# Decode step with attention and a gated MLP, forward and backward, on one core: K windows in slots of their own, transposed copies on ScalarE, larger and nested fill packets

## The chip, the cores and the metric

The kernel runs on one core of a Trainium2 chip. The time is the device time of one execution in microseconds. Before the change the median of three runs is 777.7 us (776.77 to 778.44). One more execution was profiled: it took 777.6 us, and the span of its instructions is 775.8 us.

## What is computed

One token passes through a pre-norm block, and the program returns the output and the gradients of all eight inputs.

```
h  = x + attention(layernorm(x), k_cache, v_cache) @ wo     # 16 heads, 8 KV heads, Dh 256
h2 = h + (layernorm(h) @ w_gate * layernorm(h) @ w_up) @ w_down
attention reads only the last W = 4096 of Sk = 32768 cache rows
outputs: h2, dx, dK, dV (1 x 8 x 32768 x 256 each, bf16), dwq, dwo, dw_gate, dw_up, dw_down
```

dK and dV (out_2 and out_3) are 134 MB each. Only the last 4096 rows of each of the 8 groups hold anything but zero; the other 28,672 rows of each group, 14.7 MB, are zeros, and the program has to write them. In all it moves 330 MB, and 281 MB of that are writes.

## The kernel before, in words

**The zero fills.** Everything the zeros need is a few SBUF partitions that hold zeros. `fill` (L87) writes a flat stretch of DRAM from 16 partitions (32, 36, ... 92) that are read over and over, in packets of `f` elements. All fills of whole regions are issued on SyncE, one after another, by `zero_rows_and_fills` (L108): first a piece from the zeroed tile `odd` in 8 KB packets, then the rest of out_2's first region, then 14 regions. Regions number 6 to 10 (`LONG`, L106) go in packets of `NW` = 14,336 elements, 28 KB; the others in packets of `ZW` = 8192 elements, 16 KB. The very last region (out_3, group 7) is dealt out in portions of its own. `deal(eng, e0, k, n, f)` (L97) has `k` partitions write `n` packets of `f` elements each, and `deal_all` has all 16 do so. SyncE deals three portions: 3 partitions with 14 packets of 16 KB, 16 partitions with 24 packets of 16 KB, and 16 partitions with 8 packets of 1224 elements (2448 bytes). The rest is dealt on GpSimd's queue by `deal_rest`: lap 0 once the output h2 is stored, lap 1 at the very end.

**DMA queues.** SyncE and ScalarE issue hardware-generated DMAs; SyncE's go to the queue that the profile calls q1. All loads of K, V and weights and all stores of results are issued by GpSimd, in the order written, on the software queue q0. Both queues feed the same 16 DMA engines. The framework gives hardware DMAs eight completion semaphores in turn: a DMA issued by SyncE waits until the DMA eight places before it has landed on all the engines it uses.

**Attention forward (L346 to L427).** `BIG` is one large SBUF tile cut into slots of 16 KB per partition. The V windows of groups 0 to 6 have slots 0 to 6; K windows alternate between slots 7 and 8 (`K_SLOT`, L40), and V of group 7 takes the slot of K of group 6. K of groups 0 and 1 and V of groups 0 to 2 are loaded at the start; later K windows are loaded in two halves as the slot comes free (L462). `products` (L346) transposes a window on TensorE, 8 blocks at a time, copies them from PSUM with `evac` and multiplies them by the query; `evac` (L296) alternates between ScalarE and VectorE. `moments(g)` weighs K on VectorE, multiplies on TensorE, and in between runs `scores(g+1)` and `softmax(g+1)`.

**MLP, forward and backward (L429 to L628).** The weights are loaded into slots 7 and 8; w_down comes in four pieces through a buffer of four rows. The loop at L567 turns the gradients of gate and up into rows (`to_rows`), broadcasts them (`evac`) and multiplies them with the weights on VectorE. L620 does the same for dq, with one PSUM buffer.

**dK and dV (L691 to L789).** For each group TensorE makes outer products (L764), `evac` copies them to one of the slot pairs named by `PAIR`, and GpSimd stores the pair. Stores of the weight gradients are made on the side (`during`). After the last pair GpSimd issues `deal_rest(1)`.

Of the kernel before, what the change touches and what calls it, by code (L numbers as in the profile page):

```python
# [8 lines left out]
f32 = mybir.dt.float32  # L9
# [5 lines left out]
D = 448  # L15
NI = 7
# [20 lines left out]
TAIL = 9 * SLOT  # L37
RING = TAIL + 6016
SIZE = RING
K_SLOT = [KS + g % 2 for g in range(G)]  # L40


@with_exitstack
def kernel(
# [10 lines left out]

    oT_f = const.tile([128, 32], f32)
    BIG = const.tile([128, SIZE], bf16)
    x_bf = BIG[0:1, 6 * SLOT:6 * SLOT + D]
    S_.dma_start(out=x_bf, in_=A_x.rearrange("a b d -> (a b) d"))
    go_bf = BIG[0:1, 6 * SLOT + 512:6 * SLOT + 512 + D]  # L60
    S_.dma_start(out=go_bf, in_=grad_out.rearrange("a b d -> (a b) d"))

    def flat_rows(w):
# [39 lines left out]
        fill(FILL, last[used[0]:used[0] + 16 * n * f], ALL, n, f)  # L103
        used[0] += 16 * n * f

    LONG = range(6, 11)  # L106

    def zero_rows_and_fills():  # L108
        f = NW // 4
        S_.dma_start(out=zeros[ALL, :].rearrange("p (n f) -> p n f", f=f), in_=odd[ALL, 0:f].unsqueeze(1).to_broadcast([16, 4, f]))  # L110
        fill(FILL, first[16 * NH * FH:], ALL, (FL - NH * FH) // ZW, ZW)
        for g in range(G):
            for k, o in enumerate((out_2, out_3)):
                if (g, k) not in ((0, 0), (G - 1, 1)):
                    f = NW if 2 * g + k in LONG else ZW
                    fill(FILL, region(o, g), ALL, FL // f, f)
        deal(FILL, 0, 3, 14)
        deal_all(24, ZW)
        deal_all(8, 1224)

    def deal_rest(lap):
        if lap == 0:
            deal(IO, 0, 4, 16, ZL)
            deal(IO, 4, 3, 4, ZL)
            deal(IO, 7, 2, 25, ZL)
            deal(IO, 9, 7, 10, ZL)
        else:
            deal(IO, 0, 5, 2, 512)
            deal(IO, 5, 2, 25)
            deal(IO, 7, 2, 2, 2560)  # L130
            deal(IO, 9, 7, 15)
            assert used[0] == 896 * ZW

    def slot(k):
# [35 lines left out]
    def load_V(g):  # L170
        load_window(Vw[g], A_v_cache, g)

    def load_V_half(g, h):
        t = slice(h * T // 2, (h + 1) * T // 2)
        io_load(Vw[g][:, t, :], A_v_cache[0, g, Sk - W:, :].rearrange("(p t) d -> p t d", t=T)[:, t, :])

    load_K(0)
    load_V(0)
    load_K(1)
    load_V(1)  # L180
    wd_rows = B_w_down.rearrange("(s j m) n -> j s (m n)", s=2, j=128)
    load_V(2)


    ident_bf = const.tile([128, 128], bf16)
# [110 lines left out]
    def evac(out, in_):  # L296
# [3 lines left out]
            V_.tensor_copy(out=out, in_=in_)  # L300
        evac_ctr[0] += 1

    xX = const.tile([128, NI], f32)
    V_.tensor_copy(out=xX[:], in_=rows_to_half(x_bf)[:])
    rstd1, xh1, xf1, xx1 = layernorm(xX[:], "ln1")
# [37 lines left out]
        pk_ctr[0] += 1  # L343
        return ring(k).rearrange("p (i h d) -> p i h d", i=2, h=2)

    def products(pool, x_at, vecT, g, out_ps, q):  # L346
        tr = pool.tile([128, 4, 2, 128], bf16, tag="tr", bufs=2, name="tr")
        for i in range(4):
            for dh in range(2):
                P_.transpose(tr[:, i, dh, :], x_at(g, 4 * q + i)[:, dh * 128:(dh + 1) * 128], ident_bf[:])  # L350
        xt = kt_buf()
        evac(xt, tr[:])
        for i in range(4):
            for dh in range(2):
                P_.matmul(out_ps[:, 4 * q + i, :], lhsT=xt[:, i, dh, :], rhs=vecT[:, 4 * g + dh:4 * g + dh + 3:2],  # L355
                          start=(dh == 0), stop=(dh == 1))
# [6 lines left out]
    def scores(g, q):  # L363
        if q == 0:
            sT[g] = fps.tile([128, T, 2], f32, tag="sT", bufs=2, name="sT")
        products(fps, k_at, qT, g, sT[g], q)

    def softmax(g):
        s = sT[g]
        pmax = small.tile([128, 2], f32, tag="pmax")  # L370
        V_.reduce_max(out=pmax[:], in_=s[:].rearrange("p t h -> p h t"), axis=AX)
        mt = ps.tile([2, 128], f32, tag="tmp", bufs=1)
        P_.transpose(mt[:], pmax[:], ident_f[:])
        gmax = small.tile([2, 1], f32, tag="gmax")
        V_.reduce_max(out=gmax[:], in_=mt[:], axis=AX)
        gd = small.tile([2, 2], f32, tag="gd")
        V_.tensor_scalar(out=gd[:], in0=ident_f[0:2, 0:2], scalar1=gmax[:, 0:1], scalar2=-SCALE, op0=ALU.mult, op1=ALU.mult)
        nb = ps.tile([128, 2], f32, tag="tmp", bufs=1)
        P_.matmul(nb[:], lhsT=one[0:2, 0:1].to_broadcast([2, 128]), rhs=gd[:], start=True, stop=True)
        nbias = small.tile([128, 2], f32, tag="nbias")  # L380
        V_.tensor_copy(out=nbias[:], in_=nb[:])
        e = small.tile([128, T, 2], f32, tag="ef")
        sums = small.tile([128, 2], f32, tag="psums")
        for h in range(2):
            S_.activation(out=e[:, :, h], in_=s[:, :, h], func=ACT.Exp, bias=nbias[:, h:h + 1], scale=SCALE, accum_out=sums[:, h:h + 1])
        rs = small.tile([128, 2], f32, tag="rsum")
        V_.reciprocal(out=rs[:], in_=total(sums[:], 2)[:])
        pf = small.tile([128, T, 2], f32, tag="pp", bufs=2)
        V_.tensor_tensor(out=pf[:], in0=e[:], in1=rs[:].unsqueeze(1).to_broadcast([128, T, 2]), op=ALU.mult)
        V_.tensor_copy(out=pT_all[:, g], in_=pf[:])  # L390
        p_f[g] = pf

    def moments(g):

# [3 lines left out]
        for c in range(T // 2):  # L398
# [16 lines left out]
            if g + 1 < G and 4 <= c < 12:  # L415
                with tc.issue_after(mm.ins):
                    scores(g + 1, c - 4)
                if c == 11:
                    softmax(g + 1)
            if c == 8 and g == G - 2:  # L420
                load_V_half(G - 1, 0)
            if c == 8 and g == G - 1:
                load_wo(0, 9)
        S_.copy(out=Mt[:, g, 0, :], in_=MT[0][:])
# [29 lines left out]

    bc2 = [BIG[:, o:o + F].rearrange("p (i c) -> p i c", i=2) for o in (WD0, WD0 - F)]

    for q in range(8):
        scores(0, q)
    softmax(0)
    for g in range(G):  # L460
        moments(g)
        if g + 2 < G:  # L462
            load_K(g + 2, 2)
        if g + 3 < G - 1:
            load_V(g + 3)
        if g == G - 2:
            load_V_half(G - 1, 1)
        if g == 0:

            go_f = BIG[0:1, 6 * SLOT + 1024:6 * SLOT + 1024 + 2 * D].bitcast(f32)  # L470
            V_.tensor_copy(out=go_f, in_=go_bf)
            t = ps.tile([128, D], f32, tag="tmp", bufs=1)
            P_.matmul(t[:], lhsT=one[0:1, 0:1].to_broadcast([1, 128]), rhs=go_f, start=True, stop=True)
            S_.copy(out=dh2_bc[:], in_=t[:])
    load_wo(9, 32)
    io_load(wg_sb, flat_rows(B_w_gate))

# [80 lines left out]
    for w in range(2):  # L558
        V_.tensor_tensor(out=dgu[:, w, 0:FC], in0=d_hh[:], in1=gu[:, 1 - w, :], op=ALU.mult)

    def to_rows(dst, t, cols, j0):
        for j, c in enumerate(cols):
            P_.matmul(t[:, j, :], lhsT=c, rhs=ident_bf[:, j0:j0 + t.shape[-1]], start=True, stop=True)
        evac(dst, t)

    P2 = const.tile([128, 2, NI], f32)
    for w, w_sb in ((0, wg_sb), (1, wu_sb)):  # L567
        for h in range(4):
            r = small.tile([2, HF // 4], bf16, tag="R", name="r")
            t = ps.tile([2, NI, 32], f32, tag="tmp", bufs=1, name="t")  # L570
            to_rows(r[:].rearrange("s (j m) -> s m j", m=NI), t[:], [dgu[:, w, m::NI] for m in range(NI)], 32 * h)
            for i2 in range(2):
                bc = ps.tile([128, HF // 4], f32, tag="tmp", bufs=1, name="bc")
                P_.matmul(bc[:], lhsT=Par[:, i2:i2 + 128], rhs=r[:], start=True, stop=True)
                evac(bc2[w][:, i2, h * HF // 4:(h + 1) * HF // 4], bc[:])
        wv = w_sb.rearrange("p (i c) -> p i c", i=NI)
        for i in range(NI):
            V_.tensor_tensor_reduce(out=wv[:, i, :], in0=wv[:, i, :], in1=bc2[w][:, i % 2, :], scale=1.0, scalar=0.0,
                                    op0=ALU.mult, op1=ALU.add, accum_out=P2[:, w, i:i + 1])
    dhn = const.tile([128, NI], f32)  # L580
# [7 lines left out]
    for b in range(32):  # L588
        V_.tensor_tensor_reduce(out=wg_sb[:, 0:D], in0=parked.get(b, wo_b(b)), in1=dh_bc[:], scale=1.0, scalar=0.0,  # L589
                                op0=ALU.mult, op1=ALU.add, accum_out=doW[:, b:b + 1])  # L590
    doT_f = small.tile([128, 32], f32, tag="pp", bufs=2, name="doT_f")
    V_.tensor_copy(out=doT_f[:], in_=regroup(doW[:], 1)[:])
    doT = const.tile([128, 32], bf16)
# [25 lines left out]
    rows16(doT, do_rows, 1.0)  # L619
    for b1 in range(0, 16, 4):  # L620
        r = wg_sb[0:2, b1 * 128:b1 * 128 + 512]
        t = ps.tile([2, 4, 128], f32, tag="tmp", bufs=1, name="t")
        to_rows(r.rearrange("s (b c) -> s b c", c=128), t[:], [dq[:, b:b + 17:16] for b in range(b1, b1 + 4)], 0)
        for i2 in range(2):
            bc = ps.tile([128, 512], f32, tag="tmp", bufs=1, name="bc")
            P_.matmul(bc[:], lhsT=Par[:, i2:i2 + 128], rhs=r, start=True, stop=True)
            evac(dq_bc[:, i2, b1 * 128:b1 * 128 + 512], bc[:])
    load_odd(IO)  # L628
# [92 lines left out]
    def dP(s, q):  # L721
        g = SEQ[s]
        if q == 0:
            dps[s] = bps.tile([128, T, 2], f32, tag="dp", name="dp")
        products(bps, v_at, doT, g, dps[s], q)

    def factors(s):
        R_ps = ps.tile([128, 2 * Dh], f32, tag="tmp", bufs=1)
# [94 lines left out]
```

## Time and profile before

| What | Value |
|---|---|
| Profiled execution | 777.6 us, span 775.8 us |
| Median of 3 runs | 777.7 us |
| TensorE busy | 60% of the span |
| VectorE busy | 51% |
| ScalarE busy | 20% |
| Moved by DMA | 330.09 MB, mean 425 GB/s |
| 8 KB packets on q0 (K and V halves) | 1792, median 309 ns |
| 16 KB packets on q1 | 9194, median 611 ns |
| 28 KB packets on q1 | 2688, median 1062 ns |
| Last packet of q0 ends | 769.0 us |
| Last packet of q1 ends | 774.5 us |

Times within the execution are counted from the start of the span. The packet rows come from the trace's records of single DMA packets, the others from the page. "DMA share" in a window is the mean busy share of the 16 DMA engines; it can come out at 1.01, since neighbouring packets of one engine overlap by 3 to 4 ns.

### The profile page before, as it was taken

To read this page: it belongs to the slowest core of one execution; us is meant where nothing else is said; L and a number is where in the kernel's file an instruction comes from. 1 tells how busy PE (TensorE), PEld (TensorE's weight loads), DVE (VectorE), ACT (ScalarE), POOL (GpSimd) and SP (SyncE) were. 2 spreads that over 40 slices of the span, in tenths; PEclk is the share of its full clock that TensorE was granted. 3 is DMA by queue.
4 is the path that set the end of the run, shared out by engine and by line. 5 is a ranking of instruction groups with operands and counts; after the bars stand their busy time and mean duration, and the time that the engine had idled before them with its cause. 6 is when DMAs were issued, how large, how long until landed. Compare 5 with 4: busy or idle time off the path is not lost. (4 is left out here: it accounts for less than half of the span.)

```text
span 775.8 us, 10948 instructions
## 1 busy us (share of the span) xinstructions
PE 468.8 (60%) x4427; PEld 259.6 (33%) x4472; DVE 394.3 (51%) x1179; ACT 155.5 (20%) x268; POOL 42.2 (5%) x86
## 2 busy tenths in 40 slices
PE   3899998998996423041326839686958977360000
PEld 2755565555553121020323414232313333030000
DVE  5277766766774121146683526464646756980000
ACT  0211222122110000021003414243423433130000
POOL 2000000000000000010001000000000100001000
PEclk9999999999999755555555555555555555555555
DMA  9999999999999999999999999999999999999998
GB/s 362 429 426 429 425 427 429 427 425 427 428 424 429 433 428 430 436 437 430 427 432 428 431 428 433 428 429 424 432 430 429 431 428 429 429 430 432 431 429 349
DMA packets 22803, 330.09 MB, mean 425 GB/s; under 512 B 2717, under 2 KB 2719, under 8 KB 3992
## 3 DMA queue, kind: packets, MB, share of 16 engines
q1 hardware_dynamic: 12701, 231.17, 69.6%
q0 software_dynamic: 9968, 97.77, 29.9%
q8 instruction: 35, 0.57, 0.3%
q10 hardware_dynamic: 84, 0.46, 0.1%
q14 instruction: 15, 0.12, 0.0%
HBM read 48.33 MB, written 280.59 MB: 424 GB/s over the span
## 5 line engine op out<-in xcount | busy, mean ns | idle before, releaser
L764 PE MATMUL d_ps<-BIG 32*128 32x512 bf16 x256 | 121.4, 598 | 60.2 <-ACT BIG L298 42.8
L407 PE MATMUL MT<-BIG 128*128 128x512 bf16 x467 | 134.5, 394 | 3.8 <-DMA BIG<-in_A_v_cache_dram 1.9
L403 DVE TENSOR_SCALAR BIG<-BIG,pf 128x256 bf16<-128x256 bf16 x512 | 112.6, 280 | 29.9 <-PE MT L407 25.2
L350 PE MATMUL tr<-ident_bf,BIG 128*128 128x128 bf16 x1024 | 113.5, 269 | 20.1 <-DVE doW L589 12.6
L298 ACT CAST BIG<-d_ps 128x512 bf16<-128x512 f32 x156 | 88.4, 588 | 176.8 <-PE d_ps L764 128.3
L350 PEld LDWEIGHTS <-BIG 128*128 128x128 bf16 x1024 | 81.1, 120 | 51.9 <-issue 44.1
L300 DVE COPY BIG<-tr 128x1024 bf16<-128x1024 bf16 x92 | 63.3, 688 | 50.7 <-PE tr L350 50.6
L300 DVE CAST BIG<-d_ps 128x512 bf16<-128x512 f32 x100 | 67.9, 683 | 34.8 <-DMA out_dram<-BIG 28.1
L298 ACT COPY BIG<-tr 128x1024 bf16<-128x1024 bf16 x36 | 36.4, 1012 | 131.6 <-PE tr L350 116.3
L355 PEld LDWEIGHTS <-BIG 128*128 128x128 bf16 x1024 | 36.7, 102 | 70.7 <-DVE BIG L300 44.2
L410 PEld LDWEIGHTS <-BIG 128*128 128x128 bf16 x512 | 42.1, 98 | 44.2 <-issue 8.3
L410 PE MATMUL acc<-pT_all,BIG 128*128 128x2 bf16 x512 | 44.9, 164 | 7.9 <-DVE kbar L427 6.2
L764 PEld LDWEIGHTS <-BIG 32*128 32x128 bf16 x256 | 20.7, 111 | 78.4 <-issue 59.2
L407 PEld LDWEIGHTS <-BIG 128*128 128x128 bf16 x512 | 39.0, 100 | 21.0 <-issue 8.6
L413 PE MATMUL acc<-pT_all,BIG 128*128 128x2 bf16 x512 | 44.2, 164 | 0.0
L413 PEld LDWEIGHTS <-BIG 128*128 128x128 bf16 x512 | 29.9, 96 | 0.9
L528 DVE CUSTOM_DVE_ANT_0 dh_bc<-BIG,dh_bc 128x448 bf16<-128x448 bf16 x14 | 8.7, 624 | 40.5 <-DMA BIG<-in_B_w_down_dram 40.2
L355 PE MATMUL dp<-doT,BIG 128*128 128x2 bf16 x512 | 24.2, 168 | 4.3 <-DVE BIG L300 3.4
L549 PE MATMUL y<-BIG,hh_bf 128*1 128x448 bf16 x14 | 5.9, 564 | 31.5 <-DMA BIG<-in_B_w_down_dram 30.8
L355 PE MATMUL sT<-qT,BIG 128*128 128x2 bf16 x512 | 22.1, 164 | 0.8 <-ACT BIG L298 0.6
L745 DVE TENSOR_TENSOR BIG<-r_ps,mrow 96x1024 bf16<-96x1024 bf16 (+2 forms) x15 | 18.3, 1221 | 1.0 <-PE r_ps L750 0.8
L237 PE MATMUL t<-one,xe 1*128 1x1 f32 x42 | 11.2, 333 | 12.6 <-DVE xe L236 12.6
(190 smaller groups left out, 357.4 us busy)
## 6 DMA issues: line engine op xcount, KB each, us to landing
out_dram<-zeros SPq DMA_DIRECT2D x14, 14336.0 KB, 160.5
out_dram<-BIG POOLq DMA_DIRECT2D x17, 2048.0 KB, 32.4
BIG<-in_A_v_cache_dram POOLq DMA_DIRECT2D x8, 2048.0 KB, 25.2
BIG<-in_A_k_cache_dram POOLq DMA_DIRECT2D x12, 1024.0 KB, 15.0
out_dram<-zeros SPq DMA_DIRECT2D x1, 11264.0 KB, 45.3
out_dram<-zeros SPq DMA_DIRECT2D x1, 6144.0 KB, 81.3
BIG<-in_A_k_cache_dram POOLq DMA_DIRECT2D x2, 2048.0 KB, 24.9
zeros<-in_A_wq_dram SPq DMA_DIRECT2D x1, 3584.0 KB, 15.3
```

The costliest lines, as they stand in the source:

```text
L237: P_.matmul(t[:, i:i + 1], lhsT=c, rhs=one[0:1, 0:1], start=True, stop=True)
L298: S_.copy(out=out, in_=in_)
L300: V_.tensor_copy(out=out, in_=in_)
L350: P_.transpose(tr[:, i, dh, :], x_at(g, 4 * q + i)[:, dh * 128:(dh + 1) * 128], ident_bf[:])
L355: P_.matmul(out_ps[:, 4 * q + i, :], lhsT=xt[:, i, dh, :], rhs=vecT[:, 4 * g + dh:4 * g + dh + 3:2], start=(dh == 0), stop=(dh == 1))
L403: V_.tensor_scalar(out=pk[:, i, h, :], in0=K[:, t, :], scalar1=pf[:, t, h:h + 1], scalar2=None, op0=ALU.mult)
L407: P_.matmul(MT[hf][:], lhsT=v_at(g, t)[:, hf * 128:(hf + 1) * 128], rhs=pk[:, i, :, :].rearrange("p h d -> p (h d)"), start=(t == 0), stop ...
L410: P_.matmul(acc[:, 2 * hf:2 * hf + 2], lhsT=v_at(g, t)[:, hf * 128:(hf + 1) * 128], rhs=pT_all[:, g, t, :], start=(t == 0 and hf == 0), st ...
L413: mm = P_.matmul(acc[:, 4 + dk:7 + dk:2], lhsT=K[:, t, dk * 128:(dk + 1) * 128], rhs=pT_all[:, g, t, :], start=False, stop=(t == T - 1), s ...
L528: V_.tensor_tensor_reduce(out=dh_bc[:], in0=wd_sb[:, m - m0, :], in1=dh2_bc[:], scale=1.0, scalar=0.0, op0=ALU.mult, op1=ALU.add, accum_ou ...
L745: V_.tensor_tensor(out=rows[p0:p1], in0=r_ps[p0:p1, :].unsqueeze(1).to_broadcast([p1 - p0, 8, 128]), in1=mrow[p0:p1, :].unsqueeze(2).to_br ...
L764: mm = P_.matmul(d_ps[:].rearrange("p w d -> p (w d)"), lhsT=rows[32 * k:32 * k + 32, a, :], rhs=R[32 * k:32 * k + 32, :], start=True, sto ...
```

## The change

K of groups 0 to 5 gets slots 3 to 8, one each, and is loaded whole; K of groups 6 and 7 and V of group 7 come in halves, issued in the middle of the moments of group 4, 5 and 6 and after it. x and grad_out, which share a slot at the start, move from slot 6 to slot 8. The copies of K's transposes are all made by ScalarE, as are the copies of the broadcasts of up's gradient; the multiplications there run in reverse order. The dq broadcasts get PSUM buffers of their own (two and four). Region number 5 goes in 28 KB packets. SyncE's last portion, 16 partitions with 8 packets, becomes 16 partitions with 4 packets of 1658 elements, and then 15 DMAs with 15, 14, ... 1 partitions, each with one packet of 256 + 16k elements. Lap 1 of GpSimd's portions carries the same bytes in packets of 25.6 KB and 24 KB. The numbers of elements are the same in all.

```diff
-K_SLOT = [KS + g % 2 for g in range(G)]
+K_SLOT = [3, 4, 5, 6, 7, 8, 7, 8]
...
-    LONG = range(6, 11)
+    LONG = range(5, 11)
...
         deal_all(24, ZW)
-        deal_all(8, 1224)
+        deal_all(4, 1658)
+        for k in range(15, 0, -1):
+            deal(FILL, 0, k, 1, 256 + 16 * k)
...
             deal(IO, 0, 5, 2, 512)
-            deal(IO, 5, 2, 25)
+            deal(IO, 5, 2, 16, 12800)
             deal(IO, 7, 2, 2, 2560)
-            deal(IO, 9, 7, 15)
+            deal(IO, 9, 7, 10, ZL)
...
-    load_V(2)
+    load_K(2)
...
+    def on_act(out, in_):
+        S_.copy(out=out, in_=in_)
...
-        products(fps, k_at, qT, g, sT[g], q)
+        products(fps, k_at, qT, g, sT[g], q, on_act)
...
+    LATE = {4: (Kw[6], A_k_cache, 6), 5: (Kw[7], A_k_cache, 7), 6: (Vw[7], A_v_cache, 7)}
...
+    load_V(2)
+    load_K(3)
+    load_K(4)
     for q in range(8):
         scores(0, q)
...
-        if g + 2 < G:
-            load_K(g + 2, 2)
-        if g + 3 < G - 1:
+        if g < 4:
             load_V(g + 3)
-        if g == G - 2:
-            load_V_half(G - 1, 1)
+        if g in LATE:
+            load_half(*LATE[g], 1)
...
-    for w, w_sb in ((0, wg_sb), (1, wu_sb)):
+    for w, w_sb, ev in ((0, wg_sb, evac), (1, wu_sb, on_act)):
...
-        t = ps.tile([2, 4, 128], f32, tag="tmp", bufs=1, name="t")
+        t = tps.tile([2, 4, 128], f32, tag="qt", bufs=2, name="t")
...
-            bc = ps.tile([128, 512], f32, tag="tmp", bufs=1, name="bc")
+            bc = tps.tile([128, 512], f32, tag="qb", bufs=4, name="bc")
```

More of the change, by code (lines that the diff above doesn't have):

```diff
@@ L57 @@
     BIG = const.tile([128, SIZE], bf16)
-    x_bf = BIG[0:1, 6 * SLOT:6 * SLOT + D]
+    x_bf = BIG[0:1, 8 * SLOT:8 * SLOT + D]
     S_.dma_start(out=x_bf, in_=A_x.rearrange("a b d -> (a b) d"))
-    go_bf = BIG[0:1, 6 * SLOT + 512:6 * SLOT + 512 + D]
+    go_bf = BIG[0:1, 8 * SLOT + 512:8 * SLOT + 512 + D]
     S_.dma_start(out=go_bf, in_=grad_out.rearrange("a b d -> (a b) d"))
@@ L171, in load_V, with load_half @@
         load_window(Vw[g], A_v_cache, g)
-    def load_V_half(g, h):
+    def load_half(dst, cache, g, h):
         t = slice(h * T // 2, (h + 1) * T // 2)
-        io_load(Vw[g][:, t, :], A_v_cache[0, g, Sk - W:, :].rearrange("(p t) d -> p t d", t=T)[:, t, :])
+        io_load(dst[:, t, :], cache[0, g, Sk - W:, :].rearrange("(p t) d -> p t d", t=T)[:, t, :])
     load_K(0)
@@ L344, in pk_buf, with products @@
         return ring(k).rearrange("p (i h d) -> p i h d", i=2, h=2)
-    def products(pool, x_at, vecT, g, out_ps, q):
+    def products(pool, x_at, vecT, g, out_ps, q, ev):
         tr = pool.tile([128, 4, 2, 128], bf16, tag="tr", bufs=2, name="tr")
@@ L351, in products @@
         xt = kt_buf()
-        evac(xt, tr[:])
+        ev(xt, tr[:])
         for i in range(4):
@@ L419, in moments @@
                     softmax(g + 1)
-            if c == 8 and g == G - 2:
-                load_V_half(G - 1, 0)
+            if c == 8 and g in LATE:
+                load_half(*LATE[g], 0)
             if c == 8 and g == G - 1:
@@ L461 @@
         moments(g)
-        if g + 2 < G:
-            load_K(g + 2, 2)
-        if g + 3 < G - 1:
+        if g < 4:
             load_V(g + 3)
-        if g == G - 2:
-            load_V_half(G - 1, 1)
+        if g in LATE:
+            load_half(*LATE[g], 1)
         if g == 0:
-            go_f = BIG[0:1, 6 * SLOT + 1024:6 * SLOT + 1024 + 2 * D].bitcast(f32)
+            go_f = BIG[0:1, 8 * SLOT + 1024:8 * SLOT + 1024 + 2 * D].bitcast(f32)
             V_.tensor_copy(out=go_f, in_=go_bf)
@@ L474 @@
             S_.copy(out=dh2_bc[:], in_=t[:])
+            load_K(5)
     load_wo(9, 32)
@@ L559, with to_rows @@
         V_.tensor_tensor(out=dgu[:, w, 0:FC], in0=d_hh[:], in1=gu[:, 1 - w, :], op=ALU.mult)
-    def to_rows(dst, t, cols, j0):
+    def to_rows(dst, t, cols, j0, ev=evac):
         for j, c in enumerate(cols):
             P_.matmul(t[:, j, :], lhsT=c, rhs=ident_bf[:, j0:j0 + t.shape[-1]], start=True, stop=True)
-        evac(dst, t)
+        ev(dst, t)
     P2 = const.tile([128, 2, NI], f32)
-    for w, w_sb in ((0, wg_sb), (1, wu_sb)):
+    for w, w_sb, ev in ((0, wg_sb, evac), (1, wu_sb, on_act)):
         for h in range(4):
@@ L570 @@
             t = ps.tile([2, NI, 32], f32, tag="tmp", bufs=1, name="t")
-            to_rows(r[:].rearrange("s (j m) -> s m j", m=NI), t[:], [dgu[:, w, m::NI] for m in range(NI)], 32 * h)
+            to_rows(r[:].rearrange("s (j m) -> s m j", m=NI), t[:], [dgu[:, w, m::NI] for m in range(NI)], 32 * h, ev)
             for i2 in range(2):
@@ L574 @@
                 P_.matmul(bc[:], lhsT=Par[:, i2:i2 + 128], rhs=r[:], start=True, stop=True)
-                evac(bc2[w][:, i2, h * HF // 4:(h + 1) * HF // 4], bc[:])
+                ev(bc2[w][:, i2, h * HF // 4:(h + 1) * HF // 4], bc[:])
         wv = w_sb.rearrange("p (i c) -> p i c", i=NI)
-        for i in range(NI):
+        for i in reversed(range(NI)):
             V_.tensor_tensor_reduce(out=wv[:, i, :], in0=wv[:, i, :], in1=bc2[w][:, i % 2, :], scale=1.0, scalar=0.0,
@@ L590 @@
                                 op0=ALU.mult, op1=ALU.add, accum_out=doW[:, b:b + 1])
+    tps_cm.__exit__(None, None, None)
+    tps_cm = tc.tile_pool(name="qps", bufs=1, space=bass.MemoryType.PSUM)
+    tps = tps_cm.__enter__()
     doT_f = small.tile([128, 32], f32, tag="pp", bufs=2, name="doT_f")
@@ L724, in dP @@
             dps[s] = bps.tile([128, T, 2], f32, tag="dp", name="dp")
-        products(bps, v_at, doT, g, dps[s], q)
+        products(bps, v_at, doT, g, dps[s], q, evac)
     def factors(s):
```

## The prediction

> **What bounds the kernel now.** I read the slices of the page first, then the DMA queues, then windows of the last 15 us, then what SyncE waits for. The slices:
>
> ```profile
> DMA  9999999999999999999999999999999999999998
> GB/s 362 429 426 429 425 427 429 427 425 427 428 424 429 433 428 430 436 437 430 427 432 428 431 428 433 428 429 424 432 430 429 431 428 429 429 430 432 431 429 349
> ...
> q1 hardware_dynamic: 12701, 231.17, 69.6%
> q0 software_dynamic: 9968, 97.77, 29.9%
> ```
>
> The 16 DMA engines are busy from end to end, at 424 to 437 GB/s in every slice but the first and the last. TensorE (60%) and VectorE (51%) are not the bound: whenever compute leaves the software queue (q0) empty, the zero fills on q1 take the engines. The time is therefore the packets' sum on each engine, plus some 2 us before the first packet (1.8 us by the packet records), plus what the end adds. The windows show the end (us, TensorE, its weight loads, VectorE, ScalarE, GpSimd, clock, then DMA share and GB/s):
>
> ```profile
> 765.00:767.00 2.00, 0.00 (x0) 0.00 (x0) 0.00 (x0) 0.00 (x0) 0.00 (x0) 0.50 0.98 419
> 767.00:770.00 3.00, 0.00 (x0) 0.00 (x0) 0.00 (x0) 0.00 (x0) 0.00 (x0) 0.50 0.96 410
> 770.00:771.00 1.00, 0.00 (x0) 0.00 (x0) 0.00 (x0) 0.00 (x0) 0.00 (x0) 0.50 0.89 382
> 771.00:772.00 1.00, 0.00 (x0) 0.00 (x0) 0.00 (x0) 0.00 (x0) 0.00 (x0) 0.50 0.82 342
> 772.00:773.00 1.00, 0.00 (x0) 0.00 (x0) 0.00 (x0) 0.00 (x0) 0.00 (x0) 0.50 0.45 182
> 773.00:774.00 1.00, 0.00 (x0) 0.00 (x0) 0.00 (x0) 0.00 (x0) 0.00 (x0) 0.50 0.21 83
> 774.00:775.00 1.00, 0.00 (x0) 0.00 (x0) 0.00 (x0) 0.00 (x0) 0.00 (x0) 0.50 0.03 10
> ```
>
> The share falls in steps: the engines finish one by one. Chaining the packet records engine by engine gives first end 767.1, mean 772.5, last 774.5 us; so perfect balance could save 1.9 us at most. The last three include the engines that carry SyncE's extra 3 x 14 packets. The chain of waits ends at 702.13 us with GpSimd issuing the last fills: compute is over 72 us before the end.
>
> **Packets: minus 0.4 us.** The packet records price a packet by size: 309 ns for 8 KB, 611 for 16, 912 for 24, 1062 for 28. K whole: 1792 packets of 8 KB become 768, so 512 pairs turn into 512 of 16 KB; (2 x 309 - 611) = 7 ns x 512 / 16 engines = 0.22 us. Sixth long region: 896 x 611 - 512 x 1062 = 3.7 us / 16 = 0.23. Lap 1: 25 x 611 - 16 x 950 (between the 24 and 28 KB rows) = 0.08 us on two engines, 15 x 611 - 10 x 912 = 0.05 on seven: 0.03 on average. Four loads fewer save 64 completion packets of 9 ns: 0.04. Sum 0.5; the overlap of 3 to 4 ns per packet takes a quarter back: 0.4 us.
>
> **Compute edits: nothing.** Copies of K's transposes move 32 x 688 ns from VectorE to ScalarE at 1012 ns (the rows of L300 and L298); ScalarE is at 20%. On TensorE, whose waits in the moments stage (40 to 252 us) come to 17 us, K loads account for 4.7 and V for 1.9, so earlier loads gain 7 us of compute at most. In the MLP the last copies of up's gradient no longer queue behind VectorE's products (some 8 us off the compute), and the dq buffers save some 3. Against it, the sixth long region lies beside the w_down pieces: it is next in line after the fill that landed by 289 us, and its own 16 KB packets landed by 326; VectorE waited 40.2 us for these pieces (L528). Where queues alternate, each of a piece's 8 packets per engine would wait 1062 instead of 611 ns, 3.6 us a piece, 7 to 11 in all. Compute thus moves by -18 to +11 us. Its cover is the fills: they keep the engines full either way. After the last issue the software queue still needs about 35 packets of 16 KB per engine, 21 us; only compute some 45 us later (702 to about 750) would stretch the end. The late K halves and the x slot change no engine's total either.
>
> **The last fill: plus 3.3 us.** Each SyncE DMA waits for the one eight before it. In the order of the changed program's instructions SyncE ends with 3 x 14 packets, 16 x 24, 16 x 4, then k = 15 down to 1; k = 10 waits for the 3 x 14 portion (landed at 759.5 us in the trace of before), **k = 9 waits for the 16 x 24 portion, k = 8 for the 16 x 4, k = 7 for k = 15, ... k = 1 for k = 9**. The 16 x 24 portion lands on its slowest engine at 774.05 us, the last portion at 774.85 (completion records), and the span ends at 775.8. So nine of the nested DMAs can only be issued when the fills are as good as over. SyncE's own waits show the same end:
>
> ```profile
> SPq L818 <- DMA out_dram<-zeros: 43.4, 3, 38.4
> ```
>
> Nothing is queued behind SyncE's last DMA but the end of the program, which waits for all of them. What an issue takes, no nested DMA in this trace shows; the bounds are the hardware DMAs that are not held up by a full ring:
>
> ```profile
> L61 ACTq DMA_DIRECT2D BIG<-in_grad_out_dram x1: 219/219/219, 1.3 to 1.3; - x1
> ...
> L59 ACTq DMA_DIRECT2D BIG<-in_A_x_dram x1: 520/520/520, 0.8 to 0.8; - x1
> ...
> L89 SPq DMA_DIRECT2D out_dram<-Mt x1: 654/654/654, 5.4 to 5.4; - x1
> ```
>
> Their columns are shortest, median and longest issue in ns. L61 is one packet like the k = 1 DMA and nearest, so I take 0.25 us plus a gap of 0.05; L89 (0.65) is a fill of 384 packets and the upper end. From issue to landing a small DMA takes 1.42 us: x was issued at 0.75 and landed at 2.17.
>
> Count from the landing of the 16 x 24 portion. The 16 x 4 portion behind it (4 packets of 3.3 KB, from the 99 ns row for 2.4 KB about 0.13 each) lands 0.55 later (before: 0.80 for 8 packets). k = 8 starts there, and k = 8 to 1 are eight issues: k = 1 starts at 0.55 + 7 x 0.30 = 2.65 and lands at 4.1. k = 9 has landed by 1.4, so k = 1's own wait is over. Before, the end came at 0.80: **+3.3 us**. With 0.25 us an issue, gap included, it is 0.55 + 1.75 + 1.42 - 0.80 = +2.9; with 0.65 and the gap 0.55 + 4.9 + 1.42 - 0.80 = +6.1. The lower end is +2.0, if issues cost nothing and only k = 9 and k = 1 follow each other (2 x 1.42 - 0.80). Below that the cover must come back (rival B).
>
> The Trainium skill, DMA: Bandwidth & Descriptors, Anatomy of one DMA and Rules for kernel authors, puts about 2.0 us of fixed time on a DMA, measured on the software path, and warns that transfers under 64 KB are mostly overhead, which speaks against 15 DMAs of at most 15 KB. By it, as an estimate, the last landing would be 0.6 us later than with the 1.42 us of the trace, 781.1 us in all.
>
> **Sum.** 777.6 - 0.4 + 3.3 = 780.5 us. The profiled execution (777.6) stands 0.1 under the median (777.7), so no correction.
>
> **Rivals.**
> A, the forecast: the tail is exposed, 780.5 (779.3 to 781.5 with 0.25 to 0.40 us an issue). Chance 0.50.
> B, not slower: the software queue ends last, and the nested DMAs run under it. Then only the packets count: 777.2. For it: the slower w_down pieces. Against it: q0's last packet ends at 769.0, 5 us before the fills land, and the larger packets of lap 1 take 9 rounds of 0.61 off two of its engines. It decides from compute about 9 us later than now. Chance 0.20.
> C, faster: B's cover, and the slowest engines lose work besides: one 16 KB instruction fetch (0.93 us in the packet records) that falls on another engine, or a better spread, at most 1.9 us. 777.6 - 0.4 - 0.9 to 1.9 = 775.3 to 776.3. It needs two things at once: 0.12.
> D: the issues cost as much as a large fill's, 0.65 us: 777.6 - 0.4 + 6.1 = 783.3. For it: every SyncE issue in the trace that is not held up takes 0.39 to 0.87 us; against it, L61. Chance 0.14.
> E: the change does something else than planned to the end, such as compute 45 us late or fills that run dry while SyncE waits: 785 and more. The waits eight back are over long before, all but the last nine: 0.04.
>
> The range leaves out C and E, 16 in 100: 776.6 (B, with half a microsecond of the scatter of the runs shown) to 783.4 (D). A measurement of this kernel can tell about 0.2%, 1.6 us, from no change. Slower: A and D, 0.64, and half of E, 0.66 in all; same: B, 0.20; faster: C, with the rest of E as unknown, 0.14.
>
> **What would show it.** Packets: 1024 fewer of 8 KB on q0, 384 fewer on q1; DMA busy in all slices. Tail: in the windows of the last 8 us a stretch of 3 to 4 us with a DMA share near 0, and SyncE issuing nine fill DMAs after the last large packet, each 0.2 to 0.65 us. B would show software packets until the last 2 us. The forecast is wrong if k = 9 is issued while DMA share is still 1.00, or if the engines' last large packets end over 1 us apart from 774.

## The result and the profile after

The changed kernel takes 783.03 us (median of 6 runs, 782.82 to 783.35) against 777.43 us before (6 runs, 776.77 to 778.44): ratio 1.0072, 95% interval 1.0059 to 1.0084. It is slower by 5.6 us; 2.9 were forecast. The profiled execution took 783.13 us, its span is 781.4 us.

From the page of the changed kernel, the slices and the queues:

```profile
DMA  9999999999999999999999999999999999999995
GB/s 366 422 431 427 427 428 429 425 427 428 425 429 433 426 437 431 433 430 435 429 429 429 427 432 432 431 429 425 428 429 431 430 428 430 430 431 430 431 430 222
...
q1 hardware_dynamic: 12493, 231.17, 69.1%
q0 software_dynamic: 9168, 97.77, 29.6%
```

Same bytes and fewer packets. Between the first slice and the last the rate stays at 422 to 437 GB/s (424 to 437 before); the last slice falls to 222 GB/s from 349. The last 11 us in windows (columns as in the prediction; the last two numbers are DMA share and GB/s):

```profile
770.00:771.00 1.00, 0.00 (x0) 0.00 (x0) 0.00 (x0) 0.00 (x0) 0.00 (x0) 0.50 0.87 374
771.00:772.00 1.00, 0.00 (x0) 0.00 (x0) 0.00 (x0) 0.00 (x0) 0.00 (x0) 0.50 0.81 328
772.00:773.00 1.00, 0.00 (x0) 0.00 (x0) 0.00 (x0) 0.00 (x0) 0.00 (x0) 0.50 0.36 134
773.00:774.00 1.00, 0.00 (x0) 0.00 (x0) 0.00 (x0) 0.00 (x0) 0.00 (x0) 0.50 0.12 39
774.00:775.00 1.00, 0.00 (x0) 0.00 (x0) 0.00 (x0) 0.00 (x0) 0.00 (x0) 0.50 0.02 7
...
776.00:777.00 1.00, 0.00 (x0) 0.00 (x0) 0.00 (x0) 0.00 (x0) 0.00 (x0) 0.50 0.03 9
...
779.00:780.00 1.00, 0.00 (x0) 0.00 (x0) 0.00 (x0) 0.00 (x0) 0.00 (x0) 0.50 0.01 4
```

The engines finish their large packets a little earlier than before (0.36 and 0.12 against 0.45 and 0.21 in the windows from 772 and 773). Then the DMA share stays at 0.01 to 0.03 for six microseconds. What SyncE does in them, from its timeline (start us, us, engine, operation, count), first in a window from 773.1 us, then in one from 774.1:

```profile
773.23 0.74 SPq L89 DMA_DIRECT2D out_dram<-zeros  x1
```

```profile
774.01 5.49 SPq L89 DMA_DIRECT2D out_dram<-zeros  x8
```

These are the nested DMAs with 9 and with 8 to 1 partitions, one directly behind the other: nine issues from 773.23 to 779.50. The queues in the same stretch, from 773.7 us to the end:

```profile
DMA packets 90, 0.03 MB, mean 4 GB/s; under 512 B 45, under 2 KB 90, under 8 KB 90
```

For 0.03 MB, 45 packets and as many completion marks (packets of 4 bytes), the program runs on for some six microseconds. The waits of SyncE in the whole execution:

```profile
SPq L89 <- DMA out_dram<-zeros: 31.7, 2, 19.0
...
SPq L830 <- DMA out_dram<-zeros: 0.4, 2, 0.2
```

Before, SyncE waited for the fills at the end of the program (43.4 us at L818). Now it waits for them at L89, ahead of nested DMAs, and the end of the program has only 0.4 us left to wait.

The middle has changed as well, without effect on the end. VectorE's waits for the w_down pieces (the page before, then the page after):

```profile
L528 DVE CUSTOM_DVE_ANT_0 dh_bc<-BIG,dh_bc 128x448 bf16<-128x448 bf16 x14 | 8.7, 624 | 40.5 <-DMA BIG<-in_B_w_down_dram 40.2
```

```profile
L537 DVE CUSTOM_DVE_ANT_0 dh_bc<-BIG,dh_bc 128x448 bf16<-128x448 bf16 x14 | 8.7, 624 | 47.8 <-DMA BIG<-in_B_w_down_dram 47.6
```

The pieces cost 7.4 us more. GpSimd issues its last fill at about 707 us, 5 us later than before; from 290 to 707 us the DMA share is 1.00 to 1.01 in windows of some 100 us.

### The profile page after: what moved, and what is told of

It reads as the page before. It is cut to its first block, busy times and chain, and to the rows that moved or that the text cites. A ratio compares the mean times of both kernels' runs of the same rounds, so it can differ in the third digit from the quotient of the medians.

```text
span 781.4 us, 11051 instructions
## 1 busy us (share of the span) xinstructions
PE 472.1 (60%) x4472; PEld 261.9 (34%) x4472; DVE 373.6 (48%) x1141; ACT 191.2 (24%) x306; POOL 39.9 (5%) x82
## 5 line engine op out<-in xcount | busy, mean ns | idle before, releaser
L414 PE MATMUL MT<-BIG 128*128 128x512 bf16 x512 | 144.4, 394 | 3.8 <-DMA BIG<-in_A_v_cache_dram 3.8
L410 DVE TENSOR_SCALAR BIG<-BIG,pf 128x256 bf16<-128x256 bf16 x512 | 114.2, 284 | 56.6 <-PE MT L414 52.9
L355 PE MATMUL tr<-ident_bf,BIG 128*128 128x128 bf16 x1024 | 116.1, 268 | 3.4 <-DMA BIG<-in_A_k_cache_dram 2.3
L355 PEld LDWEIGHTS <-BIG 128*128 128x128 bf16 x1024 | 81.2, 120 | 42.6 <-issue 37.5
L306 ACT COPY BIG<-tr 128x1024 bf16<-128x1024 bf16 x64 | 64.6, 1012 | 106.4 <-PE tr L355 102.3
L417 PEld LDWEIGHTS <-BIG 128*128 128x128 bf16 x512 | 44.7, 99 | 51.5 <-issue 10.9
L302 DVE COPY BIG<-tr 128x1024 bf16<-128x1024 bf16 x60 | 41.2, 687 | 40.3 <-PE tr L355 40.3
L360 PEld LDWEIGHTS <-BIG 128*128 128x128 bf16 x1024 | 37.0, 102 | 66.5 <-DVE BIG L302 35.0
L414 PEld LDWEIGHTS <-BIG 128*128 128x128 bf16 x512 | 39.2, 99 | 20.9 <-issue 6.6
L420 PEld LDWEIGHTS <-BIG 128*128 128x128 bf16 x512 | 30.0, 96 | 0.9
```

The costliest lines, as they stand in the source:

```text
L306: S_.copy(out=out, in_=in_)
L410: V_.tensor_scalar(out=pk[:, i, h, :], in0=K[:, t, :], scalar1=pf[:, t, h:h + 1], scalar2=None, op0=ALU.mult)
L414: P_.matmul(MT[hf][:], lhsT=v_at(g, t)[:, hf * 128:(hf + 1) * 128], rhs=pk[:, i, :, :].rearrange("p h d -> p (h d)"), start=(t == 0), stop ...
L417: P_.matmul(acc[:, 2 * hf:2 * hf + 2], lhsT=v_at(g, t)[:, hf * 128:(hf + 1) * 128], rhs=pT_all[:, g, t, :], start=(t == 0 and hf == 0), st ...
L420: mm = P_.matmul(acc[:, 4 + dk:7 + dk:2], lhsT=K[:, t, dk * 128:(dk + 1) * 128], rhs=pT_all[:, g, t, :], start=False, stop=(t == T - 1), s ...
```

## The experiments

All are read against runs of the kernel before on the same chip; its median there was 777.32 to 777.62 us.

**e1 and e2: all but the tail, and the tail alone.** e1 is the changed kernel with the old last portion, e2 the kernel before with the new one.

```diff
-        deal_all(8, 1224)        # before, e1
+        deal_all(4, 1658)        # after, e2
+        for k in range(15, 0, -1):
+            deal(FILL, 0, k, 1, 256 + 16 * k)
```

> The changed kernel with SyncE's last portion as before (16 partitions, 8 packets of 1224 elements) in place of the 16 x 4 portion and the 15 nested DMAs; all else as changed. Theory (nine small DMAs issued one after another once the fills have landed cost the time): the trace of after has its last 16 KB packets done 0.7 us earlier than before, so the whole comes to 777.4 - 0.6 = 776.8 us (776.2 to 777.4). Rival 1 (the K slots, the sixth long region and the ScalarE copies slow the middle, and that reaches the end): 781 or more. Rival 2 (half and half): about 780.

> The kernel before with only SyncE's last portion replaced by the 16 x 4 portion and the 15 nested DMAs. Theory: the 16 x 24 portion lands at 774.1 as before, nine issues of 0.7 us and a landing follow: 777.4 + 0.55 + 8 x 0.72 + 0.7 - 0.8 = 783.6 us (782.8 to 784.4). Rival 1 (the middle costs the time): 777 to 778.

Measured: e1 776.98 us (11 runs), ratio 0.9996 (0.9987 to 1.0004); e2 783.69 us (4 runs), ratio 1.0074 (1.0059 to 1.0088). The nested DMAs account for the whole loss, in either kernel: 783.69 - 777.36 = 6.3 us in e2, 783.03 - 776.98 = 6.1 us between after and e1. All other edits together lie within a measurement of no change. In e2's timeline, from 773.6 us, the same row stands:

```profile
773.68 6.28 SPq L89 DMA_DIRECT2D out_dram<-zeros  x9
```

**e6: twelve in place of fifteen.**

```diff
-        deal_all(4, 1658)
-        for k in range(15, 0, -1):
+        deal_all(2, 3371)
+        for k in range(15, 3, -1):
```

> The changed kernel with 12 nested DMAs (15 down to 4 partitions; the rest of the bytes in 2 packets of 3371 elements on all 16). Theory (issues after the fills have landed are paid one by one): three issues fewer, 0.72 + 0.60 + 0.41 us and three gaps of 0.04, so 783.0 - 1.9 = 781.2 us (780.7 to 781.8). Rival (a fixed price for the first one that waits, the rest overlapping): 783.0.

Measured: 781.93 us (781.57 to 782.03), 1.1 us less than after. SyncE's timeline from 773.4 us:

```profile
773.48 4.41 SPq L89 DMA_DIRECT2D out_dram<-zeros  x6
```

Six issues in 4.4 us in place of nine in 6.3: the price goes with the number, and the rival of a fixed price (783.0) falls. It fell short of the 1.9 us expected, by the traces mostly for two reasons: these issues began 0.25 us later than those of after, and the DMA that is now last (four partitions) landed 1.70 us after the start of its issue (777.25 to 778.95), where the last of after (one partition) took 1.25.

**e4 and e5: the same nested DMAs under the other queue's work.** Both move packets from SyncE's end to GpSimd's lap 1, e4 12 packets per engine, e5 48.

```diff
-        deal_all(24, ZW)                                  # SyncE; e4: 12, e5: none
+            deal_all(IO, 12, ZW)                          # GpSimd, lap 1; e5: 24, and
+            fill(IO, region(out_2, G - 1)[16 * 32 * ZW:], ALL, FL // ZW - 32, ZW)   # e5
```

> The changed kernel with all 15 nested DMAs, but 12 of the 24 packets of SyncE's 16 x 24 portion moved to GpSimd's lap 1, so that the software queue ends last. Theory (the chain of issues is the same length and costs nothing under work of the other queue): SyncE's large packets land near 766, nine issues take until 773, the software queue ends near 774: 776.8 us (776.0 to 777.8). Rival (the nested DMAs cost the engines or the end by themselves): 782 to 783.

Measured: e4 783.76 us (5 runs). This missed, and the trace says why. From 775.1 us:

```profile
775.12 6.27 SPq L89 DMA_DIRECT2D out_dram<-zeros  x9
```

The first of the nine was not issued earlier but later than in after (773.23). It waits for the 16 x 12 portion on all 16 engines, and the last of these still had hardware packets until then. On the engines that carry little of lap 1 the hardware queue was the last one as before, so there was no cover where it was needed. The traced execution is the longest of the five (785.06), and in it a single engine is late: there the 16 x 12 portion landed at 775.1, on the 15 others by 772.4. Even without it the nine issues would have begun at about 772.5 and ended some 5 us behind the software queue's last landing (774.0). e5 moves enough for every engine:

> The changed kernel with all 15 nested DMAs, and 48 packets of 16 KB per engine moved from SyncE's end to GpSimd's lap 1 (24 of the last region's 56, and the whole 16 x 24 portion), so that on every engine SyncE's large packets are done well before the software queue is. e4 moved 12 and left the slowest engine's fills landing at 775.1. Theory (the chain of nine issues costs only what nothing covers): the last portion on 16 engines lands by about 760, the issues take some 6 us, the software queue ends near 773: 776.8 us (776.0 to 778.0). Rival (the nested DMAs cost the end by themselves, covered or not): 782 to 784.

Measured: 780.34 us (780.17 to 781.38), ratio 1.0037 (1.0022 to 1.0052): between the theory's 776.8 and the rival's 782. The chain itself is now under cover. SyncE's timeline from 714 to 769 us, and the DMA share in windows:

```profile
714.17 54.41 SPq L89 DMA_DIRECT2D out_dram<-zeros  x11
```

```profile
755.00:765.00 10.00, 0.00 (x0) 0.00 (x0) 0.00 (x0) 0.00 (x0) 0.00 (x0) 0.50 1.01 429
765.00:770.00 5.00, 0.00 (x0) 0.00 (x0) 0.00 (x0) 0.00 (x0) 0.00 (x0) 0.50 0.97 416
770.00:773.00 3.00, 0.00 (x0) 0.00 (x0) 0.00 (x0) 0.00 (x0) 0.00 (x0) 0.50 0.72 296
773.00:775.00 2.00, 0.00 (x0) 0.00 (x0) 0.00 (x0) 0.00 (x0) 0.00 (x0) 0.50 0.05 8
775.00:778.60 3.60, 0.00 (x0) 0.00 (x0) 0.00 (x0) 0.00 (x0) 0.00 (x0) 0.50 0.00 0
```

All nested DMAs are issued by 768.6 us, while the engines are full. But the last packet ends at 774.2 us, and from 775.0 us on 3.6 us pass with nothing moving. In them GpSimd is still in a DRAIN instruction at the end of the program (L832; columns: shortest, median and longest in ns, then first and last start in us; the longest starts at 718.0):

```profile
L832 POOLq DRAIN  x3: 40/93/59801, 718.0 to 778.3; - x3
```

718.04 + 59.80 = 777.84 us, 2.9 us after the last software landing (774.92). The same row of the kernel before, whose longest drain starts at 701.92:

```profile
L818 POOLq DRAIN  x3: 45/102/70477, 701.9 to 775.6; - x3
```

There it ended at 772.4, 3.0 us after the software queue's last landing at 769.4, and lay under the hardware fills, which landed by 774.85.

**e10: the software queue last, without nested DMAs.** e5 with SyncE's old last portion, `deal_all(FILL, 8, 1224)`.

> e5 without the nested DMAs: SyncE's last portion as before (16 partitions, 8 packets of 1224 elements), with the same 48 packets moved to GpSimd's lap 1. In the trace of e5 GpSimd's final drain ended at 777.9, 2.9 us after the last software landing. Theory (under cover the nested DMAs cost nothing, and what e5 lost is the drain): as e5, 780.3 us (779.6 to 781.0). Rival (what e5 lost is a remainder of the nested DMAs): 777.0.

Measured: 780.46 us (779.86 to 781.37), ratio 1.0036 (1.0023 to 1.0050), as e5. So under cover the 15 nested DMAs cost nothing that can be measured (each interval is some 2 us wide), and most of what both lose is the drain. It shows here too:

```profile
L830 POOLq DRAIN  x3: 40/102/58244, 720.5 to 779.2; - x3
```

720.48 + 58.24 = 778.73 us, 2.9 us after the last software landing (775.81), and the span ends at 779.5. In e5 and e10 the span ends 3.7 us after the last software landing; before, it ended 1.0 us after the last hardware landing (774.85). The difference, 2.7 us, is the drain's part of the some 3 us by which both lie above e1 (1.0037 and 1.0036 against 0.9996). The rest is not accounted for.

**e3, e8 and e9: nested DMAs whose waits do not bind.** e3 has six of other sizes, e8 the first six of the change, e9 all 15, one after each region fill.

```diff
-        deal_all(4, 1658)
-        for k in range(15, 0, -1):
+        deal_all(7, 1166)                # e3;  e8: (7, 1091)
+        for k in range(15, 3, -2):       # e3;  e8: range(15, 9, -1)
```

```diff
                     fill(FILL, region(o, g), ALL, FL // f, f)
+                    one_nested()         # e9: the next of the 15
```

> The changed kernel with six nested DMAs in place of 15 (15, 13, 11, 9, 7 and 5 partitions; the rest of their bytes in 7 packets of 1166 elements on all 16). None of the six waits for the 16 x 24 portion. Theory (only DMAs whose wait binds cost): as without nesting, 776.8 us (776.2 to 777.6). Rival (each small DMA costs the queue its time wherever it stands): 776.8 + 6/15 of 6.2 = 779.3 us.

> The changed kernel with only the first six of its nested DMAs (15 to 10 partitions; the rest in 7 packets of 1091 elements on all 16). e3 did this with six others and came out 1.2 us over e1, which has none. Theory as it stands (a DMA whose wait does not bind is free): 777.0 us (776.4 to 777.6), and e3 owed its 1.2 us to something else. Rival (each small DMA costs 0.2 us wherever it stands): 778.2.

> The changed kernel with the same 15 nested DMAs in the same sizes, but one after each of SyncE's region fills in place of all at the end; the 16 x 4 portion stays last. No nested DMA's wait binds, and a large fill ends last. Theory (place and order cost the time, not the DMAs): as e1, 777.0 us (776.4 to 777.6). Rival, from e3 and e8, which came out 1.2 us over e1 with six nested DMAs (each costs 0.2 us wherever it stands): 780.0.

Measured: e3 778.16 us (1.0008, 0.9999 to 1.0016), e8 778.26 us (1.0008, 0.9999 to 1.0018), e9 778.31 us (1.0008, 0.9999 to 1.0017). All 15 with no binding wait cost 4.7 us less than all 15 at the end, so place and order decide. The rival of 0.2 us per DMA would have put e9 at 780.0; with 15 it comes out as with six, so "wherever it stands" falls. But all three lie above e1, by 1.2 to 1.3 us in the median (the intervals overlap a little), and above the theory's ranges.

The lowest runs tell the three apart. Those of e3 (777.57) and e8 (777.82) lie 1.0 and 1.2 us above the lowest of e1 (776.60): all their runs are shifted. The lowest of e9 (776.82) is that of the kernel before on its chip (776.83). The traces of e3 and e8 show something that fits the shift. There the six small DMAs stand behind the last fill of an engine. Their packets follow one another within 0.05 us, but their landings on one engine (the reports that its part is complete) come 0.17 to 0.22 us apart. In e8 all engines but one have ended their packets by 773.9 us, and the last landing on these is at 775.06; in e1 the last landing is at 773.86. That is 1.2 us, the size of e8's shift; so the price that e8's rival named (778.2) fits DMAs behind the last fill, though not those of e9. In e3 the same two times are 773.4 and 774.60. In e9 the last landing comes 0.4 us behind the last packet, as in e1.

Besides, in each of the three traces a single engine ends late (776.4, 775.5 and 776.0 us by the packet records, all others by 773.9). It also does so in e4 (775.2, others by 773.5 for packets above 2 KB) and in e10, which has no nested DMA (775.2, others by 773.6), and not in e1, before or after. In e3, e4 and e10 the packets chain to one of the two engines that carry the two 5 KB packets of lap 1; in e8 and e9 the records leave open which engine it is. The traced executions of e3, e4, e8 and e10 are the longest of their kernels, that of e9 the second longest, so these traces do not stand for the medians.

**e7, e11 and e12: the engines' ends.** e7 was to tell which engine ends first; e11 and e12 lighten engines that end last.

```diff
-            deal(IO, 9, 7, 10, ZL)
+            for i in range(7):
+                deal(IO, 9 + i, 1, 10, ZL + 32 * (i - 3))      # e7
...
-            deal(IO, 7, 2, 25, ZL)
+            deal(IO, 7, 2, 23, ZL)                             # e11, e12
-        deal(FILL, 0, 3, 14)
+        deal(FILL, 0, 3, 13)                                   # e12
```

> e1 with GpSimd's last portion (7 partitions with 10 packets of 24 KB) as seven DMAs of one partition each, whose packets differ by 64 bytes, so that the packet records tell which of them runs on the engine that ends first (at 766.5 us in e1, 5 us ahead of the next). Time as e1, 776.8 us.

Measured: 790.38 us (one run), 13 us over e1, and the question is not answered. The ten packets of each one-partition DMA did not stay on one engine: chained engine by engine, the packet records put them one apiece on ten engines. So the bytes landed on other engines than planned, and these ended between 763 and 787 us:

```profile
760.00:770.00 10.00, 0.00 (x0) 0.00 (x0) 0.00 (x0) 0.00 (x0) 0.50 (x1) 0.50 0.89 284
770.00:780.00 10.00, 0.00 (x0) 0.00 (x0) 0.00 (x0) 0.00 (x0) 0.00 (x0) 0.50 0.60 248
780.00:788.60 8.60, 0.00 (x0) 0.00 (x0) 0.00 (x0) 0.00 (x0) 0.00 (x0) 0.50 0.22 92
```

Bad dealing is not all of the 13 us. The packets themselves were slower: the 70 packets took 1.23 us in the median and up to 3.72, where each of the 70 of 24 KB in e1 took 0.91, and in the first of the windows above a DMA share of 0.89 moved only 284 GB/s. All ten packets of such a DMA read the same partition, now from ten engines; whether that slows them no run separates.

> e1 (the change without the nested DMAs) with two packets of 24 KB taken off each of two of the 16 engines, those that carry the 25 packets of lap 0 and the two 5 KB packets of lap 1 (23 instead of 25), and their bytes spread over all 16 in SyncE's last portion (8 packets of 1608 elements). In the traces of e3, e8, e9 and e10 one of these two engines ended last, 1.6 to 3 us after the next; in those of before, after and e1 it did not. Theory (the upper half of the runs is that engine being late): 1.8 us less on it and 0.2 more on the others: lowest as e1 (776.8), but none over 777.8; median 776.9. Rival (the scatter has another source): median and scatter as e1, 776.6 to 778.7.

> e11 with one packet of 16 KB less on the three engines of SyncE's 3 x 14 portion as well (3 x 13), those that end last in the traces of before and after, the rest again spread over all 16 (8 packets of 1800 elements). If balance is worth what the spread of the ends in e1 says (mean 772.2, last 773.5 us), 0.6 us less on these three and 0.1 more on the rest: 776.4 us (776.0 to 776.9). Rival (the last engine is another one each time): as e11.

Measured: e11 777.31 us (776.92 to 778.76), ratio 0.9999 (0.9991 to 1.0008); e12 777.31 us (776.73 to 778.50), ratio 0.9995 (0.9987 to 1.0004). Neither narrows the scatter nor beats e1: four of e11's 12 runs lie over the 777.8 that its theory allowed, and e12 misses its 776.4 by 0.9 us. In e11's trace one of the two lightened engines ends at 769.6 us and its twin, which carries as many bytes, at 773.5 or 774.5 (the records leave open which of two engines it is). But no engine's last packet set the end of that execution, the longest of its kernel (778.76 us). The last hardware landing is at 774.9 us and the last software landing at 773.4, and GpSimd's longest drain starts at 713.08:

```profile
L828 POOLq DRAIN  x3: 40/102/63127, 713.1 to 776.7; - x3
```

713.08 + 63.13 = 776.21 us, 2.8 us behind the software landing, and the span ends at 777.0, 0.8 us later, as in e5 and e10. So the drain can decide the end of a kernel whose hardware queue lands last. By the figures above, as an estimate, it does when the last software landing comes less than 2.7 us (3.7 less 1.0) before the last hardware landing; here it came 1.5 us before. Whether it makes other long runs long is not shown: each kernel has one trace.

No version in this study is clearly faster than the kernel before.

## Why the prediction was right, and where it was off

**What bounds the kernel: right.** The engines are busy in every slice, and the edits to the compute do not reach the end: e1 holds all of them and is at 0.9996. The middle moved as foreseen (w_down waits 7.4 us longer, 7 to 11 forecast; K's waits on TensorE in the moments stage, 4.7 us before, no longer stand among its waits there, V's went from 1.9 to 3.8) and stayed under the fills.

**The mechanism of the loss: right.** k = 9 waits for the 16 x 24 portion, and nine issues follow when nothing is left to move. e2 shows it alone, e5 with e10 shows that it costs nothing under cover, e6 that it goes by the number.

**The step that was mis-sized: 0.30 us for an issue.** I took it from L61 (219 ns), one packet issued by ScalarE, as nearest to the k = 1 DMA. On SyncE, in the trace of after, the nine issues take 0.74, 0.67, 0.73, 0.70, 0.71, 0.64, 0.72, 0.60 and 0.41 us; k = 1 is the cheapest and still costs nearly twice L61. From k = 8 to k = 1, 774.01 to 779.09 us, it is 0.73 us from one start to the next. k = 8 begins 0.78 us behind k = 9, held by that one's issue and not by the 16 x 4 portion's landing (0.55). The last landing comes 1.25 us after the start of k = 1 (1.42 forecast). With these values the same sum is 0.78 + 7 x 0.73 + 1.25 - 0.80 = 6.3 us in place of 3.3, and e2 measures 6.3. The 783.03 us measured lie above the forecast's own band (A, 779.3 to 781.5) and next to rival D's 783.3. D had the better row, with 0.65 us from the fills. That its total fits so closely is partly luck: its 6.1 us are 0.2 short, and in the two traces the 16 x 24 portion lands 0.8 us earlier than before (773.22 against 774.05), where 0.4 were taken off. The nearest row was the one on the same engine with the same kind of target, not the one with the same number of packets; whether the engine or the target counts, no run separates.

**Packets, minus 0.4 us: not contradicted, not resolved.** e1 against before is -0.04%, interval -0.13 to +0.04%; the forecast was -0.05%. Three figures of the working are off: 774.5 less 772.5 is 2.0 us, not 1.9; the waits of TensorE that were listed for the moments stage add up to 18.1 us, not 17; and an overlap of 3.5 ns for each of the 896 packets saved takes back 0.2 us of the 0.5, which leaves 0.3. None moves the forecast by more than 0.1 us.

**Rival B was priced wrong.** It held that with the software queue last only the packets would count, 777.2 us. e5 and e10 show 780.4: GpSimd's drain ends 2.9 us behind the last software landing, which the trace of before already held (772.4 after 769.4) and I had not read. It left out a wait that was hidden then. e4 shows a second flaw in it: cover has to exist on the slowest engine, since the wait is for all 16. In the changed kernel itself B did not come about: the software queue's last packet ends at 765.4 us.

**The fixed time of a DMA.** The last nested DMA (k = 1) landed 1.25 us after its issue began, the eight before it 1.61 to 1.81 us. The Trainium skill, DMA: Bandwidth & Descriptors, Anatomy of one DMA, puts the fixed time at about 2.0 us, for the software path. With it the sum gave 781.1 us, and the trace does not bear it out: all nine hardware DMAs took less. The Trainium skill, DMA: Bandwidth & Descriptors, Rules for kernel authors, warns that transfers under 64 KB are mostly overhead. The trace agrees where nothing covers them: nine transfers of at most 7 KB take some 6 us, most of it issuing one after another. Under cover, e5 against e10, no cost shows.

**What stays open:** why one engine ends up to 3 us late in some executions (e3, e4, e8, e9, e10) and not in others. That the nested DMAs cause it is excluded by e10, which has none. The Trainium skill, DMA: Bandwidth & Descriptors, Latency and other measured facts, says that engines 7 and 15 are usually slower than the others. The packet records do not number the engines, so no run here shows whether this is one of them. e9's median, 1.3 us above e1's, may come from that engine; its trace shows it late, but one trace does not stand for 11 runs, so this is argued and not shown. In e3 and e8 the shift of the lowest runs fits the landings 0.2 us apart, and no run varies that spacing alone.

## What to carry to other kernels

When a kernel is bound by DMA, read what comes behind the last large transfer: which waits the last few small DMAs inherit (here from the eighth DMA before), on which engine they are issued, and what still covers them. Price an issue from a row of the same engine with the same target, and remember that a wait for all 16 DMA engines ends with the slowest. Small DMAs that even out the end belong among the large ones, as in e9, and not behind the last fill, as in e8, if they are to be there at all: no version with them beat e1. A queue whose drain is slow should land well before the other.

## What the runs showed of the hardware that was not expected

- On SyncE a fill DMA of 1 to 9 packets takes 0.41 to 0.74 us to issue (0.73 us from start to start), with nothing to hold it up (after). Beside a busy software queue the last six took 1.08 to 1.11 us each (e5).
- Small DMAs that stand one behind the other on an engine land 0.17 to 0.22 us apart, though their packets follow within 0.05 us (e3, e8).
- GpSimd's final drain ended 2.8 to 3.1 us after the last software landing in all 14 traces. With the software queue last, that cost 2.7 us of the execution (e5, e10).
- A software DMA of one partition with ten packets puts one packet on each of ten engines, and its packets take 1.23 us in the median in place of 0.91 (e7).
- Two engines with the same number of bytes ended at least 3.9 us apart (e11).
